# Two of three exp readings summed by an accumulating DMA before TensorE reads them, in an attention kernel

## The chip, the core and the metric

The kernel runs on one core of a Trainium2 chip. The time is device microseconds (us) of one execution. The kernel before takes 669.34 us, the median of three runs (669.19 to 669.51).

## What is computed

A transformer block with one key and one value head for 32 query heads of 20 columns each, in parallel with a feed-forward block, over 2048 rows of 640 columns in bfloat16:

```python
xn = _layernorm(x, axis=-1)
q = (xn @ wq).reshape(B, S, H, Dh).transpose(0, 2, 1, 3)   # H = 32, Dh = 20
k = xn @ wk                                               # one head, shared
v = xn @ wv
p = _softmax(einsum("bhqd,bkd->bhqk", q, k) * Dh ** -0.5, axis=-1)
o = einsum("bhqk,bkd->bhqd", p, v).transpose(0, 2, 1, 3).reshape(B, S, H * Dh) @ wo
return x + o + einsum("bsf,fd->bsd", silu(einsum("bsd,df->bsf", xn, w1)), w2)
```

## The kernel before

**Blocks.** The scores are cut into 2048 blocks of 128 keys by 512 queries, each of them one matmul that fills one bank of PSUM (L1127, called S here). Four heads of one query chunk make a group; there are 32 groups of 64 blocks. An S step is three or four blocks at once, since TensorE runs matmuls of 32 rows beside each other in its four row strips.

**Three ways to exp.** A block is turned into exp values in one of two ways. ScalarE reads two or three neighbouring banks and writes exact exps in bfloat16 (L1161, an E block). Or VectorE turns the scores of one bank into 16-bit integers whose bits, read as bfloat16, are a rough exp (L1176, a Z block). The rough reading is made better by averaging three of them: GpSimd adds two constants to the bit patterns of up to three Z blocks at a time (L1202, 64-bit integer adds that hold four 16-bit values each), which gives two shifted readings Y0 and Y1, each weighted by its own copy of V (`PH`: shifts 0, 43, 86; weights 1.0, 0.8046875, 0.625).

**PV.** Each reading is a matmul against V (L968, called PV), into one of the four 32-column strips of the group's accumulator U, so four of them run beside each other as one set. An E block costs one PV, a rough block three: one for Z, one each for Y0 and Y1. With 732 rough blocks that is 2048 + 2 x 732 = 3512 matmuls.

**The rest.** When a group is done, VectorE copies U out of PSUM (L1245), a DMA on SyncE's queue transposes it (L1216), VectorE takes the reciprocal of the row sums (L1231) and multiplies (L1236, called the product of U). The layer norm, K and V stand at the start (V's copies are made at L1804). The feed-forward block, the query projections and the output projection are spread between the attention steps as jobs (matmuls at L870; ScalarE's tanh at L1336; VectorE's L1341, L1294, L1405, L1424). Where a projection's query rows go to their places, SyncE's queue issues small transfers (L1303).

**What sets the order.** Every engine runs a fixed list of instructions, made at build time by a list scheduler (class `Sched`). It holds a cost for each operation and a latency for each hand-over. TensorE's choice is made in `step`: an S step when enough PSUM banks are free and ScalarE is about to run out, else PV sets or jobs. A table `SEG` holds 28 numbers for each 32 or so blocks of progress (how far VectorE may be behind before it gets no more blocks, when PV is preferred, and so on). `flush_z` hands a filled triple of Z blocks to GpSimd; `normalise` makes the reciprocal and the product of U. Waits between engines are on semaphores, in the order of the lists: an engine whose next instruction waits holds up all that stand behind it. Buffers go round: 35 E blocks, 8 triples of Z, 4 pairs of triples of Y.

Of the kernel before, what the change touches and what calls it, by code (L numbers as in the profile page):

```python
# [16 lines left out]
P = 128  # L17
# [18 lines left out]
UT_LATE = 2.0  # L36
UT_LATE1 = 4.0
# [8 lines left out]
PH = ((0, 1.0), (43, 0.8046875), (86, 0.625))  # L46
# [4 lines left out]
NBLK = 35  # L51
NZ = 8
NY = 4
QS = 6
ZB = 3
# [49 lines left out]
YP_FIX = 0.147  # L105
YP_BLK = 0.218
# [13 lines left out]
            "ACT4", "SPLIT", "U2", "LOOK", "W4", "M3")  # L120
SEG = (
# [105 lines left out]
class Sched:  # L227
# [59 lines left out]
    def ready(self, op, extra=0.0):  # L287
# [17 lines left out]
        if op.lock:  # L305
            r = max(r, self.lock_end["pool" if op.eng == "dve" else "dve"])
# [1576 lines left out]
```

## Time and profile before

One execution was profiled. Its own time is 669.12 us; the span from its first to its last instruction is 667.3 us, so 1.8 us lie around it, and it stands 0.22 us below the median.

| what | value |
|---|---|
| median of three runs | 669.34 us |
| the profiled execution | 669.12 us, span 667.3 us |
| first exp starts, last exp ends | 18.51 us, 654.08 us |
| busy: TensorE, ScalarE, VectorE, GpSimd | 659.4, 647.7, 601.3, 404.6 us |
| PV matmuls, S matmuls | 3512, 2048 |
| blocks exped by ScalarE, by VectorE | 1316, 732 |
| integer adds on GpSimd | 492 |

In the tables of the profile, PE is TensorE (PEld its weight loads), DVE VectorE, ACT ScalarE, POOL GpSimd and SP SyncE. A group's row reads: line, engine, operation, output from input, shapes, count, then busy time and the mean duration of one, then the engine's idle time before them and what ended it. Instructions on one engine overlap by their pipelines, so the mean duration is longer than the step from one to the next. The chain of waits is followed back from the last instruction; a row of it is start, length, and what ran.

### The profile page before, as it was taken

How to read it: one execution, taken by the hardware profiler on the slowest of the kernel's cores; microseconds unless marked ns; L12 is line 12 of the kernel's file. 1: busy time of each engine (PE TensorE's matmuls, PEld its weight loads, DVE VectorE, ACT ScalarE, POOL GpSimd, SP SyncE). 2: the span in 40 equal slices, each digit the busy share in tenths (PEclk: the TensorE clock that was granted, in tenths of full speed). 3: DMA queues.
4: the chain of work that ended last, by engine and by line, in shares of the span. 5: the costliest groups of instructions: out<-in, count | busy, mean ns of one | idle time of the engine just before them, and what ended most of it. 6: DMA issues, size and time to landing. Idle time of an engine off the chain costs nothing.

```text
span 667.3 us, 22800 instructions
## 1 busy us (share of the span) xinstructions
PE 659.4 (99%) x9735; PEld 220.4 (33%) x9735; DVE 601.3 (90%) x1085; ACT 647.7 (97%) x737; POOL 404.6 (61%) x509
## 2 busy tenths in 40 slices
PE   8999999999999999999999999999999999999998
PEld 4432233332323322233333323233233333223345
DVE  7888999999989999999889999988999999998783
ACT  7999999999999999999999999999999999999993
POOL 2056457777486656676556653866767674676550
PEclk9999999999999999999999999999999999999999
DMA  7565201010012210000003110000002121001001
GB/s 211 110 213 150 73 14 12 2 26 2 18 44 62 57 10 17 3 10 18 19 10 84 41 32 17 10 10 18 10 13 47 38 57 37 10 10 31 5 11 41
DMA packets 51433, 26.73 MB, mean 40 GB/s; under 512 B 38566, under 2 KB 50694, under 8 KB 51334
## 3 DMA queue, kind: packets, MB, share of 16 engines
q1 hardware_dynamic: 51190, 25.12, 14.5%
q8 instruction: 78, 1.28, 0.8%
q14 instruction: 21, 0.17, 0.1%
q10 hardware_dynamic: 144, 0.16, 0.1%
HBM read 11.44 MB, written 2.62 MB: 21 GB/s over the span
## 4 chain that ended last, share of the span: by engine, by line
PE 87%; ACT 7%; DVE 3%; SPq 1%; DMA 1%; issue 0%; ACTq 0%
PE psall L968 33%; PE psall L1127 28%; PE psall L870 26%; ACT sbt L1161 6%; DVE sbt L1176 2%; ACT sbt L1336 1%; SPq L1531 1%; DMA sbt<-in_A_x_dram 1%; DVE sbt L1424 0%; PE psall L1326 0%; DVE sbt L1236 0%; ACT sbt L1620 0%; DVE sbt L1666 0%; DVE sbt L1771 0%; ACT sbt L1655 0%
## 5 line engine op out<-in xcount | busy, mean ns | idle before, releaser
L1161 ACT ACTIVATE sbt<-psall 128x1024 bf16<-128x1024 f32 (+2 forms) x649 | 620.1, 1129 | 3.5 <-PE psall L1127 2.6
L1202 POOL INT64_ADD sbt<-sbt x492 | 399.7, 827 | 244.4 <-DVE sbt L1176 171.3
L1176 DVE TENSOR_SCALAR sbt<-psall 128x512 uint16<-128x512 f32 x732 | 473.1, 683 | 46.3 <-PE psall L1127 37.1
L968 PE MATMUL psall<-sbt 128*32 128x512 bf16 x3512 | 265.0, 383 | 0.2
L1127 PE MATMUL psall<-sbt 32*128 32x512 bf16 x2048 | 245.8, 384 | 2.1 <-ACT sbt L1161 0.7
L870 PE MATMUL psall<-sbt 128*32 128x320 bf16 (+2 forms) x3923 | 220.7, 331 | 0.5 <-DVE sbt L1176 0.4
L1127 PEld LDWEIGHTS psall<-sbt 32*128 32x128 bf16 x2048 | 61.9, 91 | 241.4 <-ACT sbt L1161 161.1
L870 PEld LDWEIGHTS psall<-sbt 128*32 128x32 bf16 x3923 | 84.6, 95 | 84.6 <-issue 54.4
L968 PEld LDWEIGHTS psall<-sbt 128*32 128x32 bf16 x3512 | 64.4, 95 | 101.3 <-issue 64.6
L1336 ACT ACTIVATE sbt<-psall 128x512 bf16<-128x512 f32 x54 | 39.6, 739 | 0.0
L1341 DVE SCALAR_TENSOR_TENSOR sbt<-sbt,psall 128x512 bf16<-128x512 bf16 x54 | 36.6, 682 | 2.6 <-ACT sbt L1336 1.2
L1245 DVE CAST sbt<-psall 128x512 bf16<-128x512 f32 x32 | 21.8, 681 | 5.4 <-PE psall L968 5.3
L1236 DVE TENSOR_TENSOR sbt<-sbt 128x320 bf16<-128x320 bf16 x31 | 18.3, 591 | 0.1
L846 PE MATMUL psall<-sbt 128*128 128x512 bf16 (+4 forms) x55 | 15.2, 428 | 1.2 <-DVE sbt L1590 1.2
L1424 DVE SCALAR_TENSOR_TENSOR sbt<-psall,sbt 128x320 bf16<-128x320 f32 x28 | 13.1, 477 | 2.9 <-PE psall L870 2.9
L1405 DVE SCALAR_TENSOR_TENSOR sbt<-psall,sbt 128x320 bf16<-128x320 f32 x28 | 13.5, 483 | 1.6 <-PE psall L870 1.4
L1294 DVE TENSOR_SCALAR sbt<-psall 128x512 bf16<-128x512 f32 (+1 forms) x19 | 12.9, 680 | 0.1
L1635 DVE BATCH_NORM_STATS2 sbt<-sbt 128x6 f32<-128x320 bf16 x22 | 10.0, 470 | 0.9 <-DMA sbt<-in_A_x_dram 0.7
L1421 ACT ACTIVATE sbt<-psall 128x320 bf16<-128x320 f32 x4 | 1.7, 438 | 8.7 <-PE psall L870 8.7
L846 PEld LDWEIGHTS psall<-sbt 128*128 128x128 bf16 x55 | 5.5, 109 | 9.1 <-issue 4.0
L1231 DVE RECIPROCAL sbt<-sbt 128x16 f32<-128x16 bf16 x31 | 7.5, 243 | 0.0
L1620 ACT ACTIVATE sbt<-sbt 128x640 bf16<-128x640 bf16 x5 | 3.6, 730 | 3.2 <-DMA sbt<-in_A_x_dram 3.2
(57 smaller groups left out, 70.1 us busy)
## 6 DMA issues: line engine op xcount, KB each, us to landing
sbt<-in_A_x_dram SPq DMA_DIRECT2D x32, 160.0 KB, 3.2
out_dram<-sbt SPq DMA_DIRECT2D x15, 160.0 KB, 2.0
sbt<-in_B_w_dram SPq DMA_DIRECT2D x5, 432.0 KB, 5.3
sbt<-sbt SPq DMA_DIRECT2D x105, 20.0 KB
sbt<-in_B_w_dram SPq DMA_DIRECT2D x13, 160.0 KB, 3.1
sbt<-sbt SPq DMA_TRANSPOSE x58, 2.5
sbt<-in_A_wo_dram SPq DMA_DIRECT2D x5, 160.0 KB, 3.1
sbt<-in_A_wq_dram SPq DMA_DIRECT2D x5, 140.0 KB, 3.1
```

The costliest lines, as they stand in the source:

```text
L846: return pe.matmul(self.bk(b, 0, n), self.zero[:, 0:P], self.zero[:, 0:n], start=True, stop=True)
L870: ins = pe.matmul(self.bk(b, 0, n, r, r + SLOT), w[:, r:r + SLOT], x, start=start, stop=stop, tile_position=(0, r), skip_group_check=True)
L968: ins = pe.matmul(self.bk(ub[k], 0, QW, r, r + SLOT), self.v[:, it.w, it.kt, :], it.x(), start=f, stop=False, tile_position=(0, r), skip_g ...
L1127: ins = pe.matmul(self.bk(bank[x]), self.kT[r:r + SLOT, kt * P:(kt + 1) * P], self.qT[r:r + SLOT, g % QS, :], start=True, stop=True, tile_ ...
L1161: return a.activation(self.E[:, b0 * QW:(b0 + na) * QW].rearrange("p (b n) -> p b n", n=QW), src, AF.Exp, scale=ACT_SCALE)
L1176: return v.tensor_scalar(self.Z[:, zs, zp * QW:(zp + 1) * QW], self.bk(bb), OFF, ZMAX, ALU.add, ALU.min)
L1202: sc.new("pool", YP_FIX + YP_BLK * n, lambda g, k=k: g.int64_add(self.Y[:, ys, k, 0:w].bitcast(I64), self.Z[:, zs, 0:w].bitcast(I64), PH[k ...
L1236: sc.new("dve", t_dve_ps(16 * DH), lambda v: v.tensor_tensor(dst, ut[:, :, :, 0:DH], rb, ALU.mult), [key, ("rL", up)], [("o", h0 + i) for ...
L1245: sc.new("dve", t_dve_ps(QW), lambda v: v.tensor_copy(self.U[:, up, :], self.bk(ub)), [("B", ub)], [("U", up)], prio=U_PRIO, name=f"Uev{g}")
L1336: sc.new("act", t_act(QW), lambda a: a.activation(t, src, AF.Tanh, scale=0.5), [("B", b)], [("tb", tp)], prio=TH_PRIO, name=f"th{c}_{fk}") ...
L1341: sc.new("dve", t_dve_ps(QW), lambda v: v.scalar_tensor_tensor(out=self.hT[0:rows, fk, :], in0=t, scalar=1.0, in1=src, op0=ALU.add, op1=AL ...
L1405: sc.new("dve", t_dve_ps(320), lambda v: v.scalar_tensor_tensor(out=in1, in0=ps, scalar=0.5, in1=in1, op0=ALU.mult, op1=ALU.add), [("B", b ...
```

## The change

Four things change together, and the lists are planned anew with a new table.

1. **Two copies of V.** The shifts become 39 and 82, and both shifted readings have the same weight (`VW = (1.0, 0.71875)`), so Y0 and Y1 are used with the same copy of V. VectorE makes two copies instead of three.
2. **Merged triples.** For full triples where GpSimd is planned to be less than `MG` us behind (a number of the table, 0 to 4), after 78 us and not near the end of a group, GpSimd issues a DMA that adds Y1 to Y0 in place, in bfloat16, 384 KB at a time. TensorE then reads one sum instead of Y0 and Y1: three matmuls instead of six for the triple. The scheduler counts 0.9 us for the issue, 5.7 us from the start of the issue to the landing, and 0.28, 0.22 and 0.12 us more for the three adds behind it.
3. **The product of U kept apart from GpSimd.** The product waits by semaphore for GpSimd's last add, GpSimd's next add waits for the product, and the scheduler holds GpSimd back when a product is about to be ready.
4. **Other numbers.** Later due times for U's transposes (2.0 to 3.8 us) and for the query transfers (+1.8 us); 36 E blocks, 6 triples of Z, 5 pairs of triples of Y; the table's 64 rows get new numbers and a 29th column.

```diff
-PH = ((0, 1.0), (43, 0.8046875), (86, 0.625))
+SHIFT = (39, 82)
+VW = (1.0, 0.71875)
+NRM = 0.42
+ACC_ISSUE = 0.9
+ACC_LAND = 5.7
+ACC_NEXT = (0.28, 0.22, 0.12)
+ACC_FROM = 78.0
+ACC_DMA = 1.8
+MG_END = 16
-UT_LATE = 2.0
+UT_LATE = 3.8
-NBLK = 35
-NZ = 8
-NY = 4
+NBLK = 36
+NZ = 6
+NY = 5
 SEG = (
-    (6.04, 3.723, 0.711, 0.248, 4, 4, 5, 1.38, 0.05, 0, 2.56, 6, 2.29, 0.4, 10, 6, 6, 54, 15, 31, 2, 0, 0, 1, 99, 0, 0, 1),
+    (4.38, 0.382, 0.113, 0.226, 4, 5, 1, 1.298, 0.05, 4.33, 2.053, 16, 2.57, 1.281, 10, 6, 10, 54, 15, 33, 8, 0, 0, 3, 99, 0, 0, 1, 2),
...
@@ commit
             if e == "dve":
                 self.last_add = op
-            self.lock_end[e] = op.end + (0.2 if e == "dve" else 0.0)
+                if op.name[:3] == "nrm" and self.last_pool is not None and self.last_pool.end > start - KEEP:
+                    op.deps.add(self.last_pool)
+            elif not op.dma:
+                self.last_pool = op
+            self.lock_end[e] = op.end + (0.2 if e == "dve" else 0.5 if op.dma else 0.2)
@@ flush_z
+        merge = n == ZB and back < MG and sc.t["pe"] > ACC_FROM and self.bp < GB * (g1 + 1) - MG_END
         for k in range(2):
-            sc.new("pool", YP_FIX + YP_BLK * n, lambda g, k=k: g.int64_add(
+            yp = sc.new("pool", YP_FIX + YP_BLK * n, lambda g, k=k: g.int64_add(
...
+            yp.lock = True
+        if merge:
+            op = sc.dma("pool", lambda g: g.dma_start(
+                self.Y[:, ys, 0, 0:w].bitcast(BF16), self.Y[:, ys, 1, 0:w].bitcast(BF16), accum_op=ALU.add),
+                [("Y", ys, 1, i) for i in range(n)], [("Y", ys, 0, i) for i in range(n)], P * w * 2,
+                sem=self.acc_sem[ys], prio=3.9, name="acc")
...
         for i, (t, g, kt, j) in enumerate(self.zblocks):
-            for k in range(2):
-                self.item(g, j, kt, k + 1, lambda k=k, i=i: self.Y[:, ys, k, i * QW:(i + 1) * QW].bitcast(BF16),
-                          [("Y", ys, k, i)])
+            for k in range(1 if merge else 2):
+                self.item(g, j, kt, 1,
+                          lambda k=k, i=i: self.Y[:, ys, k, i * QW:(i + 1) * QW].bitcast(BF16), [("Y", ys, k, i)])
```

In the code of the change S is at L1160, PV at L1001, the jobs at L903, ScalarE's exps at L1194, the Z blocks at L1209, the adds at L1238, the new DMA at L1244, the product of U at L1287. The list of each engine shows what moved. Counted over the whole lists: 96 triples are merged; VectorE has 736 blocks instead of 732; PV is 2048 + 2 x 736 - 3 x 96 = 3232 matmuls; ScalarE exps 1312 blocks, in 634 instructions of two banks, 9 of three and 17 of one (before: 565, 51 and 33); the S steps are 641 runs instead of 626; GpSimd has 502 adds (472 of a full triple) instead of 492; fill matmuls that only keep TensorE warm (L846) go from 55 to 49.

GpSimd's list from the first small triples on (a triple is 128x768, two blocks 128x512, one 128x256), before:

```order
L1202 ISA sbt<-sbt 128x768 x14
L1750 MEMSET sbt 128x640
L1202 ISA sbt<-sbt 128x768 x8
L1202 ISA sbt<-sbt 128x256 x2
L1202 ISA sbt<-sbt 128x768 x30
L1202 ISA sbt<-sbt 128x512 x2
```

And the same place of the changed program:

```order
L1238 ISA sbt<-sbt 128x768 x12
L1803 MEMSET sbt 128x640
L1238 ISA sbt<-sbt 128x768 x10
L1238 ISA sbt<-sbt 128x256 x2
L1238 ISA sbt<-sbt 128x768 x10
L1244 DMA sbt<-sbt 128x1536
L1238 ISA sbt<-sbt 128x768 x4
L1238 ISA sbt<-sbt 128x512 x2
```

Where GpSimd had adds alone, a DMA issue now stands behind the second add of a merged triple, and later adds queue behind it.

TensorE's list around the first merged triple, changed program. The first row is the S step that gave VectorE the last of the triple's three blocks; the last row begins with the matmul that waits for the DMA's landing:

```order
L1160 MATMUL psall<-sbt 128x512 x3
L1001 MATMUL psall<-sbt 32x512 x8
L1160 MATMUL psall<-sbt 128x512 x3
L1001 MATMUL psall<-sbt 32x512 x8
L1160 MATMUL psall<-sbt 128x512 x4
...
L1160 MATMUL psall<-sbt 128x512 x3
L1001 MATMUL psall<-sbt 32x512 x16
L1160 MATMUL psall<-sbt 128x512 x4
L1001 MATMUL psall<-sbt 32x512 x8
```

Between the two stand ten S steps and nine runs of PV or jobs with 22 sets of four.

The end of TensorE's list, from the last S step on (32x320 matmuls at L870 or L903 are the feed-forward and output projections), before:

```order
L1127 MATMUL psall<-sbt 128x512 x2
L968 MATMUL psall<-sbt 32x512 x18
L870 MATMUL psall<-sbt 32x320 x8
L968 MATMUL psall<-sbt 32x512 x2
L870 MATMUL psall<-sbt 32x320 x20
L968 MATMUL psall<-sbt 32x512 x2
L870 MATMUL psall<-sbt 32x320 x28
L1252 MATMUL psall<-sbt 128x128 x4
L870 MATMUL psall<-sbt 32x320 x56
L1368 MATMUL psall<-sbt 128x128 x4
L870 MATMUL psall<-sbt 32x320 x176
```

And changed:

```order
L1160 MATMUL psall<-sbt 128x512 x4
L1001 MATMUL psall<-sbt 32x512 x25
L903 MATMUL psall<-sbt 32x320 x16
L1001 MATMUL psall<-sbt 32x512 x2
L903 MATMUL psall<-sbt 32x320 x32
L1304 MATMUL psall<-sbt 128x128 x4
L903 MATMUL psall<-sbt 32x320 x40
L1421 MATMUL psall<-sbt 128x128 x4
L903 MATMUL psall<-sbt 32x320 x88
```

The same matmuls exist in all, but 112 of the 288 projection matmuls that stood behind the last S step now stand ahead of it.

In VectorE's list, 30 of the 31 products of U now wait for GpSimd's semaphore as well; before, none did. Of the Z blocks one waits for GpSimd to have read its buffer.

More of the change, by code (lines that the diff above doesn't have):

```diff
@@ L35 @@
 UBANK = 7
-UT_LATE = 2.0
-UT_LATE1 = 4.0
+UT_LATE = 3.8
+UT_LATE1 = 5.0
 BANKS = (6, 0, 1, 2, 3, 4, 5)
@@ L45 @@
 OFF = 16045.0
-PH = ((0, 1.0), (43, 0.8046875), (86, 0.625))
+SHIFT = (39, 82)
+VW = (1.0, 0.71875)
+NRM = 0.42
+NRM_SOON = 0.3
+NRM_PRIO = -2.0
+ACC_ISSUE = 0.9
+ACC_LAND = 5.7
+ACC_RATE = 165e3
+ACC_NEXT = (0.28, 0.22, 0.12)
+ACC_FROM = 78.0
+ACC_DMA = 1.8
+MG = 3.0
+MG_END = 16
 ZMAX = 32512.0
@@ L104 @@
 Y0_COST = 1.3294
-YP_FIX = 0.147
-YP_BLK = 0.218
+YP_FIX = 0.159
+YP_BLK = 0.222
 LIB = 0.2
@@ L119 @@
             "ZWAIT", "Y0_POOL", "Y0_COST", "JOB_BURST", "TILE_CAP", "E_HIGH", "Q_LEAD", "U_GO", "U_Z", "JU_E", "STRETCH",
-            "ACT4", "SPLIT", "U2", "LOOK", "W4", "M3")
+            "ACT4", "SPLIT", "U2", "LOOK", "W4", "M3", "MG")
 SEG = (
[64 rows of a table removed]
[64 rows of a table added]
 )
@@ L244, in __init__ @@
         self.dmaq = defaultdict(float)
+        self.after_acc = 99
+        self.last_pool = None
     def sem(self, name):
@@ L306, in ready @@
             r = max(r, self.lock_end["pool" if op.eng == "dve" else "dve"])
+            if op.eng == "pool":
+                for d in self.pend["dve"]:
+                    if d.lock and d.name[:3] == "nrm" and all(x.avail is not None and x.avail <= self.t["pool"] + NRM_SOON
+                                                              for x in d.deps):
+                        r = max(r, self.t["dve"] + d.dur)
         return r
@@ L312, in commit @@
             op.on_pick(op)
+        if e == "pool":
+            if op.dma:
+                self.after_acc = 0
+            else:
+                if self.after_acc < len(ACC_NEXT):
+                    op.dur += ACC_NEXT[self.after_acc]
+                self.after_acc += 1
         op.start = start
@@ L319, in commit @@
             else:
-                op.avail = max(op.end + 2.0, q + op.mode / 375e3) + op.late
+                op.avail = max(op.end + 2.0, q + op.mode / (ACC_RATE if op.name == "acc" else 375e3)) + op.late
             self.dmaq[e] = max(q, op.avail - op.late)
@@ L518, in alloc @@
         self.kT = sb([P, S], BF16)
-        self.v = sb([P, 3, KT, SLOT], BF16)
+        self.v = sb([P, 2, KT, SLOT], BF16)
         self.qT = sb([P, QS, QW], BF16)
@@ L594, in steps_init @@
         self.yset = 0
+        self.merged = 0
+        self.acc_no = [0] * NY
+        self.acc_sem = [self.sc.sem(f"acc{i}") for i in range(NY)]
         self.zblocks = []
@@ L1200, in flush_z @@
         w = n * QW
+        g1 = self.zblocks[-1][1]
+        back = max(sc.t["pool"] - sc.t["pe"], 0.0) + sum(o.dur for o in sc.pend["pool"])
+        merge = n == ZB and back < MG and sc.t["pe"] > ACC_FROM and self.bp < GB * (g1 + 1) - MG_END
         for k in range(2):
-            sc.new("pool", YP_FIX + YP_BLK * n, lambda g, k=k: g.int64_add(
+            yp = sc.new("pool", YP_FIX + YP_BLK * n, lambda g, k=k: g.int64_add(
                 self.Y[:, ys, k, 0:w].bitcast(I64), self.Z[:, zs, 0:w].bitcast(I64),
-                PH[k + 1][0] * 0x0001000100010001), zk + [("lib",)], [("Y", ys, k, i) for i in range(n)],
+                SHIFT[k] * 0x0001000100010001), zk + [("lib",)], [("Y", ys, k, i) for i in range(n)],
                 prio=4.0, name=f"yp{k}")
+            yp.lock = True
[4 more added lines that the diff above has]
+                sem=self.acc_sem[ys], prio=3.9, name="acc")
+            op.dur = ACC_ISSUE
+            op.lock = True
+            op.late = ACC_LAND - 2.0 - ACC_ISSUE
+            self.acc_no[ys] += 1
+            op.inc_no = self.acc_no[ys]
+            self.merged += 1
+            for _, g, kt, j in self.zblocks:
+                self.nz[g][j] -= 0.5
         for i, (t, g, kt, j) in enumerate(self.zblocks):
-            for k in range(2):
-                self.item(g, j, kt, k + 1, lambda k=k, i=i: self.Y[:, ys, k, i * QW:(i + 1) * QW].bitcast(BF16),
-                          [("Y", ys, k, i)])
+            for k in range(1 if merge else 2):
+                self.item(g, j, kt, 1,
+                          lambda k=k, i=i: self.Y[:, ys, k, i * QW:(i + 1) * QW].bitcast(BF16), [("Y", ys, k, i)])
             self.g_late[g] -= 1
@@ L1235, in normalise @@
         rb = bass.AP(self.rL, rl.offset, [list(rl.ap[0]), list(rl.ap[1]), [1, 4], [0, DH]])
-        sc.new("dve", t_dve_ps(16 * DH), lambda v: v.tensor_tensor(
+        last = g == self.NG - 1
+        op = sc.new("dve", NRM, lambda v: v.tensor_tensor(
             dst, ut[:, :, :, 0:DH], rb, ALU.mult), [key, ("rL", up)], [("o", h0 + i) for i in range(4)],
-            prio=U_PRIO if g < self.NG - 1 else -1.0, name=f"nrm{g}")
+            prio=-1.0 if last else NRM_PRIO, name=f"nrm{g}")
+        op.lock = not last
         self.norm_made[g // 8] += 4
@@ L1306, in consume @@
                 ops[-1].dur = 0.74
+                ops[-1].late = ACC_DMA if sc.t["pe"] > ACC_FROM else 0.0
             sc.note(ops[-1], (), [("q", c, h, lo) for h in heads])
@@ L1597, in prologue @@
         pool(1.4, lambda g: g.memset(self.v[:, :, :, :], 0.0), [("idb",), ("id2",)], [("v0",)] + [("v", i) for i in range(8)])
-        for k in range(3):
-            pool(0.15, lambda g, k=k: g.memset(self.v[:, k, :, DH:DH + 1], 0.5 * PH[k][1]), [("v0",)],
+        for k in range(2):
+            pool(0.15, lambda g, k=k: g.memset(self.v[:, k, :, DH:DH + 1], 0.5 * VW[k]), [("v0",)],
                  [("v0",)] + [("v", i) for i in range(8)])
@@ L1802, in consume @@
                 sv = self.bk(b, 0, 20 * m).rearrange("p (i d) -> p i d", d=DH)
-                for k in range(3):
+                for k in range(2):
                     sc.new("dve", 0.07 + m * DH / 960.0, lambda v, k=k: v.tensor_scalar(
-                        self.v[:, k, n0:n1, 0:DH], sv, PH[k][1], None, ALU.mult),
+                        self.v[:, k, n0:n1, 0:DH], sv, VW[k], None, ALU.mult),
                         [("B", b), ("v0",)], [(kk, i) for i in range(n0 // 2, n1 // 2) for kk in ("v", "vv")], prio=0.6,
```

126 rows, old and new, of the table SEG are left out of this document.

## The prediction

> **What bounds the kernel now.** I read the page first, then the chain of waits, then the groups by form, then the windows. The page's first lines show no single bound:
>
> ```profile
> span 667.3 us, 22800 instructions
> PE 659.4 (99%) x9735; PEld 220.4 (33%) x9735; DVE 601.3 (90%) x1085; ACT 647.7 (97%) x737; POOL 404.6 (61%) x509
> PE 87%; ACT 7%; DVE 3%; SPq 1%; DMA 1%; issue 0%; ACTq 0%
> ```
>
> TensorE is busy 99% and carries 87% of the chain. Busy time of pipelined matmuls says little, so I look at pieces of the chain near the end, and at two others (start, length, what ran):
>
> ```profile
> 18.51 18.32 ACT sbt L1161 x18
> 253.80 12.83 ACT sbt L1161 x14
> ...
> 645.20 0.55 PE psall L968 x8
> 646.07 0.98 PE psall L968 x16
> 647.92 0.32 PE psall L1127 x3
> 648.24 0.76 PE psall L968 x12
> 651.61 0.32 PE psall L1127 x2
> 655.81 2.02 PE psall L870 x56
> ```
>
> From 8 to 12 to 16 PV matmuls the run grows by 0.21 and 0.22 us: a set of four costs 0.216, and changing to it and back to S adds about 0.11 to a run. An S step of two or three blocks costs 0.32 whatever is in it. A set of the 320-column jobs costs 2.02 / 14 = 0.144. These pieces follow each other without a pause, so TensorE really is full where the chain lies on it. It is not alone:
>
> ```profile
> L1161 ACT ACTIVATE sbt<-psall 128x1024 bf16<-128x1024 f32 x565 | 543.3, 1112 | 2.4 <-PE psall L1127 1.4 <-PE psall L968 0.3
> L1161 ACT ACTIVATE sbt<-psall 128x1536 bf16<-128x1536 f32 x51 | 76.3, 1526 | 1.1 <-PE psall L1127 1.1
> 57.12 0.63 ACT L1336 ACTIVATE sbt<-psall 128x512 bf16<-128x512 f32 x1
> 57.60 2.90 ACT L1161 ACTIVATE sbt<-psall 128x1024 bf16<-128x1024 f32 x3
> 563.07 1.12 ACT L1161 ACTIVATE sbt<-psall 128x1024 bf16<-128x1024 f32 x1
> 563.97 0.70 ACT L1336 ACTIVATE sbt<-psall 128x512 bf16<-128x512 f32 x1
> 642.93 11.15 ACT L1161 ACTIVATE sbt<-psall 128x1536 bf16<-128x1536 f32 x12 [0.50 <-PE psall L1127]
> 78.00:628.00 550.00, 548.96 (x8159) 175.27 (x8157) 510.61 (x859) 547.71 (x609) 359.65 (x443) 1.00 0.10 24
> ```
>
> The last row is the window from 78 to 628 us: PE, PEld, DVE, ACT and POOL busy, granted clock, DMA share. ScalarE is busy 547.71 of 550. But one exp lasts 1112 ns while the next may start after 0.90 (563.07 to 563.97), so a delay of up to 0.2 us between two hides under the tail of the first. At start-to-start costs of 0.90 for two banks, 0.48 for one (57.12 to 57.60) and 0.90 + (1526 - 1112) ns = 1.32 for three, the exps and tanhs need 565 x 0.90 + 51 x 1.32 + 33 x 0.48 + 54 x 0.48 = 617.5 us. They take from 18.51 to 642.93 + 11.15 = 654.08, that is 635.6: some 18 us of hidden room. Not all can be had: where the chain lies on ScalarE itself it runs 14 in 12.83, 0.916 each, 1.8% above 0.90, which is 11 us over 617. So 7 us of ScalarE's time is won by a quicker TensorE, at most. Two engines are full together, with VectorE at 510.61 of 550 as a near third. GpSimd has 190 us to spare in that window.
>
> **The change part by part.** *PV.* 96 merged triples take 288 matmuls out, four more blocks on VectorE put 8 in. By the runs in the two lists, sets of four fall from 889 to 828: 61 x 0.216 = -13.2 us. But the S steps grow from 626 runs to 641, each 0.32 and a turn of 0.11: 15 x 0.43 = +6.5. Six fills less: -1.3. TensorE's sum: -8.0 us.
>
> *ScalarE.* 634 x 0.90 + 9 x 1.32 + 17 x 0.48 + 54 x 0.48 = 616.6, so -0.9 us: the change hardly takes work from it. Behind the last S step, where ScalarE has nothing left, 112 of 288 projection matmuls are gone, 28 sets x 0.144 = -4.0, against 5 more PV matmuls, +0.3. So ScalarE's path (start, exps, end) is shorter by 0.9 + 3.7 = 4.6 us if its hidden room stays as it is; the projections that moved forward run beside exps, and are in TensorE's sum.
>
> *VectorE.* The rows:
>
> ```profile
> L1176 DVE TENSOR_SCALAR sbt<-psall 128x512 uint16<-128x512 f32 x732 | 473.1, 683 | 46.3 <-PE psall L1127 37.1
> L1236 DVE TENSOR_TENSOR sbt<-sbt 128x320 bf16<-128x320 bf16 x31 | 18.3, 591 | 0.1
> L1236 DVE TENSOR_TENSOR sbt<-sbt x31: 471/483/1072, 60.8 to 640.3; 128x320 bf16<-128x320 bf16 x31
> L1804 DVE TENSOR_SCALAR sbt<-psall 128x80 bf16<-128x80 f32 x12 | 2.8, 233 | 0.1
> L1202 POOL INT64_ADD sbt<-sbt x492 | 399.7, 827 | 244.4 <-DVE sbt L1176 171.3 <-PE psall L968 69.5 <-PE psall L1127 1.6
> PEld psall L968 <- POOL sbt L1202: 15.9, 69, 0.3
> ```
>
> Four blocks more cost 4 x 0.65 = +2.6, four copies of V less give 0.9. The product of U has median 483 and mean 591 ns, up to 1072: some of the 31 are stretched, and kept apart they give 31 x 0.108 = -3.3 us. The new wait costs between nothing (GpSimd is already idle) and one add of 0.83 each, 26 us, and while VectorE waits, Z blocks queue behind it, and TensorE's next S step behind the banks they hold. The scheduler holds GpSimd back for a coming product, so I take a fifth, +5. VectorE's sum is +3, inside the 39 us it has free in the window, spread thin.
>
> The Trainium skill (SBUF — State Buffer, Who interferes with whom) states that a VectorE operation with two SBUF inputs and a GpSimd operation that reads SBUF exclude each other for a whole instruction, whichever is second. The longest product, 1072 ns, is 0.59 above the median and so less than one whole add of 0.83; by the rule alone each collision would cost up to 0.83 and the parting would give up to 26 us rather than 3.3. I stay with the row.
>
> *GpSimd and the merge.* The trace has no DMA issued by GpSimd and none that adds. The nearest rows:
>
> ```profile
> L1303 SPq DMA_DIRECT2D sbt<-sbt x135: 558/707/1261, 44.4 to 565.4; - x135
> sbt<-sbt SPq DMA_DIRECT2D x1, 512.0 KB, 3.7
> sbt<-in_B_w_dram SPq DMA_DIRECT2D x13, 160.0 KB, 3.1
> L1216 SPq DMA_TRANSPOSE sbt<-sbt x31: 1189/1209/1976, 55.3 to 636.2; - x31
> DMA to landing us min/median/max: 2.3/2.4/4.1
> 565.93 11.25 POOL L1202 INT64_ADD sbt<-sbt  x14 [6.01 <-PE psall L968]
> 566.72 9.81 DVE L1176 TENSOR_SCALAR sbt<-psall 128x512 uint16<-128x512 f32 x15
> ```
>
> An issue is 0.56 to 1.26 us on SyncE's queue: 96 of them are 54 to 121 us of GpSimd's time, beside its 190 free, so GpSimd does not become the bound. I count them at the scheduler's 0.9. Plain transfers of 160 and 512 KB land in 3.1 and 3.7 us; 384 KB would take 3.5, of which about 0.65 grows with size. An adding transfer also reads its destination: at least that growing part again, 4.1; at four times it, 5.4. So, from the S step: its 0.39, the Z block 0.68, two adds 2 x 0.80 (14 in 11.25), issue 0.9, landing 3.5 to 5.4, in all 7.1 to 9.0 us, and small waits between. TensorE's work from that step to the first reader, for the triple in the list: 10 S steps and 22 sets at 0.216, 19 turns of 0.105, is 8.9 us; by the same count over all 96 the median is 9.6, the tightest tenth under 7.8, the least 7.2. So a landing up to about 5 us costs nothing but at the tightest tenth: at 5.4 ten readers wait 1 us, +10. A landing at the plain price costs nothing. I take 4.1 to 5, and +1 us for the tight ones.
>
> The Trainium skill (DMA: Bandwidth & Descriptors, Anatomy of one DMA) gives GpSimd-issued transfers 2.0 us plus bytes at 436 per ns, an estimate of 2.9 us for 384 KB. By it no reader would wait; nothing there prices the adding, and no row of the trace before shows it.
>
> *Transposes and queries.* They share the DMA engines with 96 x 384 KB. U's transpose lands in 2.4 us (median), and the reciprocal behind it is in VectorE's list; it now stands 1.8 us later by plan. Nothing if the delay is under that.
>
> **The sum.** If TensorE decides everywhere, -8.0; if ScalarE with its room unchanged, -4.6. Both are full, and the chain changes between them. Tail and -0.9 are sure to both; in the middle TensorE has -4.3 to give and ScalarE 7 us of room to take it. I take -7.0, seven tenths of the way from the one to the other, and +1 for late merges: -6.0. The profiled 669.12 becomes 663.1, and with its 0.22 below the median 663.3 us.
>
> **Rivals.**
> *ScalarE alone.* Its room is jitter, no effect of TensorE, and the new lists are no better at the turns: -4.6 and the +5 of VectorE's waits shows in part, so 665 to 669. For it: only 0.9 us of its work goes. Against: 87% of the chain is TensorE.
> *Late merges (slower).* The adding transfer, or one behind the queries' transfers, lands later than the lists expect, in order-bound TensorE. It decides from a landing of about 5.5 us after the issue. Merges come about every 5.7 us and a window from S to reader is 9.6 us, so 56 windows follow each other in 540 us: each us beyond costs up to 56, at half of the windows 28. With 1 us late: 663 + 28 = 691; with only the tightest tenth late, 673. Against: today TensorE waits at most 0.3 us for an add, 15.9 in all.
> *Starved issue.* If VectorE's Z blocks, which run nearly without a pause, kept GpSimd from issuing, each issue would wait for one or more of them, 0.65 us each, and the landing would slip past the readers as above: 680 to 700. Against: 14 adds at 0.80 ran beside 15 Z blocks back to back, so Z blocks block no write of GpSimd. The Trainium skill (SBUF — State Buffer, SBUF: two separate sides) warns of such a thing: GpSimd cannot write a DMA's descriptors while VectorE runs an operation that holds the port they share. The row speaks against its being met here.
> *VectorE's new waits.* U's transposes come late by 1 us, or products wait a whole add: 31 us against 39 free; a quarter shows, 663 + 8 = 671.
> That nothing is merged is ruled out by the list: 96 issues stand in it.
>
> **How the numbers follow.** Forecast 0.68 (659 to 667); ScalarE alone 0.12, of which 0.05 is within 0.2%; late merges 0.12; starved issue 0.03; VectorE's waits 0.05, split 0.01 faster, 0.03 same, 0.01 slower. About 0.2%, 1.3 us, is what a measurement of this kernel can tell. Faster: 0.68 + 0.07 + 0.01 = 0.76. Same: 0.08. Slower: 0.12 + 0.03 + 0.01 = 0.16. The low end takes TensorE's -8.0 with VectorE's 3.3 shown as well, 658. The high end takes in VectorE's waits and stops short of late merges, 672; some 0.13 lies above it.
>
> **What would show it.** Right: PV 3232 in some 244 us busy; exps from 18.5 to about 651.5; behind the last S step 9 instead of 12.5 us; products of U near 0.48 each; waits of weight loads at PV for the DMA under 5 us in all. Wrong: a row of PV waiting for the merge with tens of us; GpSimd's adds with many waits behind the issue; reciprocals waiting for transposes; ScalarE with idle time of over 10 us.

## The result and the profile after

The changed kernel takes 664.51 us (median of four runs, 663.79 to 664.74), the kernel before, timed beside it, 669.42 (669.19 to 669.51). The ratio is 0.9925, with a 95% interval of 0.9913 to 0.9937: 4.9 us less, where 6.0 less was forecast. The profiled execution took 664.74 us, 4.38 less than the profiled one of before.

The page's first lines and the shares of the chain, after:

```profile
span 662.9 us, 22421 instructions
PE 652.1 (98%) x9446; PEld 215.2 (32%) x9449; DVE 601.2 (91%) x1085; ACT 645.8 (97%) x748; POOL 488.0 (74%) x614
PE 61%; ACT 35%; DVE 2%; DMA 1%; SPq 0%; issue 0%
```

TensorE's share of the chain fell from 87% to 61%, and ScalarE's rose from 7% to 35%. That reads as if TensorE had got some room; the experiments below show that this reading is only half right.

Where the 4.4 us of span went can be read from ScalarE's first and last exp (start, length, what ran):

```profile
18.61 1.02 ACT L1194 ACTIVATE sbt<-psall 128x1024 bf16<-128x1024 f32 x1 [1.09 <-PE psall L1160]
637.74 15.35 ACT L1194 ACTIVATE sbt<-psall 128x1024 bf16<-128x1024 f32 x16
```

The exps ran from 18.51 to 654.08 before, 635.6 us, and run from 18.61 to 637.74 + 15.35 = 653.09 now, 634.5 us: 1.1 less. From there to the end of the span it was 667.3 - 654.1 = 13.2 us and is 662.9 - 653.1 = 9.8. So three quarters of the gain lie behind the last exp. The windows of just that stretch, first of before (columns: window, its length, then PE, PEld, DVE, ACT and POOL busy with their instructions, granted clock, DMA share, GB/s):

```profile
654.08:667.30 13.22, 10.16 (x276) 7.36 (x270) 6.08 (x14) 1.69 (x5) 0.00 (x0) 1.00 0.15 52
```

And after:

```profile
653.08:662.90 9.82, 6.77 (x173) 4.79 (x170) 5.17 (x12) 1.70 (x5) 0.00 (x0) 1.00 0.19 68
```

TensorE runs 103 matmuls less there and is busy 3.39 us less: this is the whole of the 3.40 us by which the stretch is shorter. The stretch repeats: in the profiles of the runs below that leave the end alone it is 13.2 to 13.4 us with the old lists and 9.8 with the new ones. By the medians (4.9 us) some 1.5 us are then left for all that stands ahead, where the two profiled executions show 1.0; the profiled one of after is the slowest of its four, the only one with a granted clock below 1.00 (0.997), and the clock stands at 0.66 between 25 and 30 us in it. The middle, 78 to 628 us, hardly changed; after:

```profile
78.00:628.00 550.00, 548.00 (x8069) 175.31 (x8061) 510.67 (x863) 547.09 (x618) 440.90 (x544) 1.00 0.47 91
```

TensorE 548.0 against 549.0, ScalarE 547.1 against 547.7, VectorE 510.7 against 510.6. GpSimd is the one that took on work, 81 us, and the DMA engines' share went from 0.10 to 0.47.

The groups that the change touches (line, engine, operation, count, then busy and mean ns, then idle before them and what ended it):

```profile
L1194 ACT ACTIVATE sbt<-psall 128x1024 bf16<-128x1024 f32 (+1 forms) x660 | 617.9, 1105 | 4.8 <-PE psall L1160 4.4
L1238 POOL INT64_ADD sbt<-sbt x502 | 428.5, 975 | 123.6 <-DVE sbt L1209 87.3
L1209 DVE TENSOR_SCALAR sbt<-psall 128x512 uint16<-128x512 f32 x736 | 478.8, 684 | 42.1 <-PE psall L1160 32.6
L1001 PE MATMUL psall<-sbt 128*32 128x512 bf16 x3232 | 250.6, 383 | 0.4 <-DVE sbt L1394 0.4
L1244 POOL DMA_DIRECT2D sbt<-sbt x96 | 88.1, 918 | 39.1 <-DVE sbt L1287 29.4
L1287 DVE TENSOR_TENSOR sbt<-sbt 128x320 bf16<-128x320 bf16 x31 | 14.9, 481 | 0.0
```

And what waits for what at the new places (waiting engine and line, releaser, us in total, times, longest):

```profile
POOL sbt L1238 <- DVE sbt L1287: 29.7, 16, 3.0
POOL sbt L1244 <- DVE sbt L1287: 29.4, 14, 3.1
PEld psall L1001 <- POOL sbt L1238: 6.1, 27, 0.2
```

No row has PV (L1001) waiting for the adding transfer. One row has other work of TensorE waiting for another transfer, a transpose of the attention output (L1408, on SyncE's queue), once, at 515 us; before, no matmul of the jobs (L870) waited for a DMA:

```profile
PE psall L903 <- DMA sbt<-sbt: 1.2, 1, 1.2
```

The product of U starts without idle time (0.0 in its row); the price of keeping it apart is paid by GpSimd, which waits 29.7 + 29.4 us for it. The transfers themselves, from their issue to their landing:

```profile
L1244 POOL DMA_DIRECT2D sbt<-sbt x96: 827/874/1330, 81.9 to 640.3; - x96
...
DMA to landing us min/median/max: 3.8/4.3/6.2
```

### The profile page after: what moved, and what is told of

Its sections match the earlier page's. It is cut to its first block, busy times and chain, and to the rows that moved or that the text cites. A ratio compares the mean times of both kernels' runs of the same rounds, so it can differ in the third digit from the quotient of the medians.

```text
span 662.9 us, 22421 instructions
## 1 busy us (share of the span) xinstructions
PE 652.1 (98%) x9446; PEld 215.2 (32%) x9449; DVE 601.2 (91%) x1085; ACT 645.8 (97%) x748; POOL 488.0 (74%) x614
## 3 DMA queue, kind: packets, MB, share of 16 engines
q0 software_dynamic: 13824, 37.75, 30.7%
## 4 chain that ended last, share of the span: by engine, by line
PE 61%; ACT 35%; DVE 2%; DMA 1%; SPq 0%; issue 0%
ACT sbt L1194 32%; PE psall L1001 23%; PE psall L1160 20%; PE psall L903 17%; ACT sbt L1389 3%; DMA sbt<-sbt 1%; DVE sbt L1688 1%; DMA sbt<-in_A_x_dram 1%; PE psall L1379 0%; DVE sbt L1209 0%; DVE sbt L1719 0%; SPq L1584 0%; DVE sbt L1477 0%; DVE sbt L1824 0%; DVE sbt L1394 0%
## 5 line engine op out<-in xcount | busy, mean ns | idle before, releaser
L1194 ACT ACTIVATE sbt<-psall 128x1024 bf16<-128x1024 f32 (+1 forms) x660 | 617.9, 1105 | 4.8 <-PE psall L1160 4.4
L1238 POOL INT64_ADD sbt<-sbt x502 | 428.5, 975 | 123.6 <-DVE sbt L1209 87.3
L1209 DVE TENSOR_SCALAR sbt<-psall 128x512 uint16<-128x512 f32 x736 | 478.8, 684 | 42.1 <-PE psall L1160 32.6
L1160 PE MATMUL psall<-sbt 32*128 32x512 bf16 x2048 | 252.2, 385 | 2.5 <-DVE sbt L1839 1.1
L1001 PE MATMUL psall<-sbt 128*32 128x512 bf16 x3232 | 250.6, 383 | 0.4 <-DVE sbt L1394 0.4
L903 PE MATMUL psall<-sbt 128*32 128x320 bf16 (+2 forms) x3923 | 225.9, 333 | 1.4 <-DMA sbt<-sbt 1.2
L1160 PEld LDWEIGHTS psall<-sbt 32*128 32x128 bf16 x2048 | 63.2, 91 | 246.0 <-ACT sbt L1194 184.1
L1244 POOL DMA_DIRECT2D sbt<-sbt x96 | 88.1, 918 | 39.1 <-DVE sbt L1287 29.4
L903 PEld LDWEIGHTS psall<-sbt 128*32 128x32 bf16 x3923 | 82.5, 95 | 88.1 <-issue 57.5
L1001 PEld LDWEIGHTS psall<-sbt 128*32 128x32 bf16 x3232 | 60.1, 95 | 94.0 <-issue 70.2
L1287 DVE TENSOR_TENSOR sbt<-sbt 128x320 bf16<-128x320 bf16 x31 | 14.9, 481 | 0.0
L879 PE MATMUL psall<-sbt 128*128 128x512 bf16 (+4 forms) x46 | 12.5, 421 | 1.6 <-DVE sbt L1643 1.2
L1458 DVE SCALAR_TENSOR_TENSOR sbt<-psall,sbt 128x320 bf16<-128x320 f32 x28 | 13.4, 480 | 0.2 <-PE psall L903 0.2
```

Source lines behind the costliest of these rows:

```text
L879: return pe.matmul(self.bk(b, 0, n), self.zero[:, 0:P], self.zero[:, 0:n], start=True, stop=True)
L903: ins = pe.matmul(self.bk(b, 0, n, r, r + SLOT), w[:, r:r + SLOT], x, start=start, stop=stop, tile_position=(0, r), skip_group_check=True)
L1001: ins = pe.matmul(self.bk(ub[k], 0, QW, r, r + SLOT), self.v[:, it.w, it.kt, :], it.x(), start=f, stop=False, tile_position=(0, r), skip_g ...
L1160: ins = pe.matmul(self.bk(bank[x]), self.kT[r:r + SLOT, kt * P:(kt + 1) * P], self.qT[r:r + SLOT, g % QS, :], start=True, stop=True, tile_ ...
L1194: return a.activation(self.E[:, b0 * QW:(b0 + na) * QW].rearrange("p (b n) -> p b n", n=QW), src, AF.Exp, scale=ACT_SCALE)
L1209: return v.tensor_scalar(self.Z[:, zs, zp * QW:(zp + 1) * QW], self.bk(bb), OFF, ZMAX, ALU.add, ALU.min)
```

## The experiments

The theories: **TensorE decides** (its freed time is the gain), **ScalarE decides** (its work and the end are the gain, the rest is jitter), **both are full together** (each hides most of what the other gains). The last three runs ask whether a gain is paid back by the transfers, and what the semaphores are worth.

| run | what is different | us | ratio to before (95%) |
|---|---|---|---|
| after | the change | 664.51 | 0.9925 (0.9913-0.9937) |
| b_pv_cut | before, 58 PV sets cut | 667.87 | 0.9978 (0.9968-0.9988) |
| b_act_cut | before, 16 exps halved | 668.08 | 0.9982 (0.9973-0.9992) |
| b_both_cut | before, both | 664.70 | 0.9932 (0.9915-0.9948) |
| a_act_cut | after, 16 exps halved | 664.55 | 0.9928 (0.9910-0.9946) |
| a_both_cut | after, 52 PV sets and 16 exps | 660.29 | 0.9864 (0.9850-0.9879) |
| b_tail_cut | before, 28 sets before the last transposes | 668.01 | 0.9976 (0.9967-0.9986) |
| b_tail2_cut | before, 22 sets of the last row | 667.24 | 0.9966 (0.9953-0.9979) |
| b_fill | before, 33 sets more | 672.90 | 1.0050 (1.0035-1.0065) |
| a_fill | after, 31 sets more | 669.95 | 1.0012 (1.0002-1.0021) |
| a_no_dma | after without the transfers | 663.88 | 0.9914 (0.9899-0.9928) |
| a_no_lock | after without the semaphore waits | 682.72 | 1.0205 (1.0160-1.0251) |
| a_no_lock_no_dma | after without both | 664.08 | 0.9931 (0.9911-0.9950) |

**One engine relieved, in the kernel before.** 58 sets of PV in the middle become one matmul of 32 columns each:

```diff
+        cut = self.npv % 14 == 0 and 78 < sc.t["pe"] < 640 and not any(first)
...
+            if cut:
+                it, k = items[-1]
+                r = it.tile * SLOT
+                return pe.matmul(self.bk(ub[k], 0, 32, r, r + SLOT), self.v[:, it.w, it.kt, :], it.x()[:, 0:32], ...)
```

> The kernel before with its lists unchanged; 58 PV sets between 78 and 640 us, one in 14, do a single matmul of 32 columns in place of up to four of 512 (those readings are left out). That takes 58 x 0.19 = 11 us from TensorE in the middle and nothing from ScalarE, VectorE or the end. If TensorE sets the pace in the middle (the prediction's step, which let it give 2 to 4 us of its 4.3 there): -4 to -11 us. If ScalarE's list does, with its 15 us of hidden room being jitter at the hand-overs: 0 to -1.5 us.

And 16 exps of two banks read one bank:

```diff
+            short = na == 2 and self.nex > 70 and self.nex % 36 == 0
...
+                if short:
+                    return a.activation(self.E[:, b0 * QW:(b0 + 1) * QW], self.bk(run[0]), AF.Exp, scale=ACT_SCALE)
```

> The kernel before with its lists unchanged; 16 of the two-bank exps, spread from about 85 us on, exp one bank only (the other 16 blocks keep old values): 16 x 0.43 = 6.8 us less of ScalarE, the same TensorE. If ScalarE sets the pace in the middle: -4 to -7 us. If TensorE does: 0 to -2 us. Both engines full: in between, and then less than half.

11 us taken from TensorE (58 x 0.19; its busy time fell by 7.1) gave 1.4; 6.8 us taken from ScalarE (16 x 0.43; busy 4.1 less) gave 1.2. Each engine alone gives a tenth to a fifth of what it is relieved of. The chain of b_pv_cut:

```profile
ACT 63%; PE 30%; DVE 5%; issue 1%; DMA 1%; SPq 0%
```

The bound passed from TensorE to ScalarE after little more than one us. In b_act_cut the chain stayed where it had been:

```profile
PE 87%; ACT 7%; DVE 4%; DMA 1%; SPq 0%; issue 0%
```

**Both relieved, before and after.** The same two edits together (in the changed kernel 52 sets, since it has fewer):

> The kernel before with unchanged lists and both cuts at once: 58 PV sets reduced to one matmul of 32 columns (11 us less of TensorE) and 16 two-bank exps to one bank (6.8 us less of ScalarE). Alone they gave 1.4 and 1.2 us. If the two engines are full together and each alone hides behind the other, both at once give far more than 2.6: -5 to -6.5 us (ScalarE's cut nearly whole). If a third, VectorE with its order-bound list, holds both: -2 to -3 us.

> The changed kernel with unchanged lists and both cuts (52 PV sets, 10 us of TensorE; 16 exps, 6.8 us of ScalarE). Full together: -4 to -6.5 us against 664.5, about 659. A third engine as the bound: 0 to -2 us, 662.5 to 664.5.

Before, 4.6 us: somewhat under the 5 to 6.5 expected, but 2.0 more than the two single gains together. After, 4.2 us, to 660.29. The changed kernel with ScalarE alone relieved:

> The changed kernel with its lists unchanged and the same cut of 16 two-bank exps to one bank, 6.8 us less of ScalarE. If ScalarE sets the pace there (its chain share rose from 7% to 35%): -5 to -7 us against the changed kernel's 664.5, about 658.5. If TensorE still did: 0 to -2 us. In either case the cut should be worth more here than in the kernel before, since TensorE has 8 us less to do.

It gave nothing that can be measured (664.55 against 664.51; its four runs lie between 663.17 and 666.05), where more than in the old kernel had been expected, and the chain swung back to TensorE:

```profile
PE 84%; ACT 11%; DVE 1%; DMA 1%; SPq 1%; issue 0%; ACTq 0%
```

So in the old kernel both engines are full together. In the changed one the cuts show that ScalarE alone does not set the pace; the cut of PV alone was not run there. That ScalarE is still as full rests on its 35% of the chain and its 547.1 busy us of 550, and is argued, not shown. Even both cuts bring less than the smaller of them (4.6 and 4.2 us of 6.8): what comes third, VectorE or the fixed lists, was not tried.

**The end.** Two runs cut projection sets behind the last S step of the old kernel to 32 columns, first 28 sets from the rows ahead of the last transposes, then 22 sets in the last row of TensorE's list. The edit of the second (the first picks its jobs by other names):

```diff
+        if self.bp >= NB and job.name[:3] in ("G2_", "G3_", "F12", "F13") and begun:
+            self.ncut = getattr(self, "ncut", 0) + 1
+            cut = self.ncut <= 22
...
+        if self.cut and not start:
+            n, x = 32, x[:, 0:32]
```

> The kernel before with its lists unchanged; 28 of the 72 sets of projection matmuls behind the last S step do 32 columns in place of 320 (their other columns are left out), about 28 x 0.11 = 3 us less of TensorE where nothing else runs. Both theories: -2.5 to -3.5 us; under -1.5 us the end would not be TensorE's, and the gain of the change would have to come from the middle.

> The kernel before with unchanged lists; 22 of the 44 sets of projection matmuls in the last row of TensorE's list, behind the last transpose of the attention output, do 32 columns in place of 320 (the rest is left out): 22 x 0.107 = 2.35 us less. These stand where the changed kernel has 22 sets fewer. If the end is what the change won: -2.2 to -2.5 us. If something else (the last outputs' VectorE work or transfers) ends the kernel: 0 to -1 us, as the cut ahead of that transpose gave -1.3 of 3.0.

The first took 3.0 us of work out and gave 1.3, less than the 2.5 to 3.5 expected. Its timeline says why (start, length, what ran, idle before it and its releaser):

```profile
643.50 11.14 ACT L1174 ACTIVATE sbt<-psall 128x1536 bf16<-128x1536 f32 x12 [0.50 <-PE psall L1140]
...
654.70 0.39 PE L981 MATMUL psall<-sbt 128*32 128x512 bf16 x2 [0.41 <-ACT sbt L1174]
...
655.88 0.40 PE L1265 MATMUL psall<-sbt 128*128 128x128 bf16 x4 [0.50 <-DVE sbt L1258]
```

TensorE, with less to do, waits 0.41 us for the last exp and 0.50 for VectorE's copy: those sets were cover for the chain exp, PV, U, transposes. The last exp ends at 643.50 + 11.14 = 654.64, 0.56 us later than in the profile of before; these exps began 0.57 us later, so the difference lies ahead of the cut. Counted from there the end is 1.6 us shorter (13.2 to 11.6). The second cut took some 2.35 us from behind that chain and gave 2.0 (2.4 in its profile, 13.2 to 10.8). So work in TensorE's last row counts about in full, and work ahead of it by about half.

**TensorE given more.** Sets of four 320-column matmuls with zero weights are put between PV runs in the middle, about as much work as the moved projections:

```diff
+        more = self.npv % 23 == 0 and 78 < sc.t["pe"] < 640 and not any(first) and len(items) == 4
...
+                    ins = pe.matmul(self.bk(ub[items[0][1]], 0, 320, r, r + SLOT), self.zero[:, 0:SLOT], self.zero[:, 0:320], ...)
```

> The kernel before with unchanged lists and 33 additional sets of four 320-column matmuls with zero weights, behind PV sets between 78 and 640 us: 33 x 0.135 = 4.5 us more of TensorE, the sum is unchanged. It prices what it would have cost to move projections of the end (28 sets in the change) into the middle without merging. If TensorE is as full as ScalarE: +3 to +4.5 us. If ScalarE alone sets the pace and TensorE's room takes it: +0 to +1 us.

> The changed kernel with unchanged lists and 31 such sets, 4.2 us more of TensorE. The changed kernel's chain lies 35% on ScalarE, and its PV cut and exp cut together gave 4.2 us where the exp cut alone gave nothing, so I expect TensorE nearly as full: +1.5 to +3 us against 664.5. If the merges left TensorE with room in the middle: 0 to +1 us; if it is as full as before: as much as in the kernel before, +3 to +4.2.

33 sets, 4.5 us, cost the old kernel 3.5. 31 sets, 4.2 us, cost the changed one 5.4 (its ten runs lie between 668.34 and 671.52). The room of 4 us that the sum had found for TensorE in the middle is not there to be filled: the changed kernel is at least as sensitive as the old one. That it costs more than the sets last, and more than was expected in any case, is explained in part by its profile (671.23 us). The transpose that held TensorE for 1.2 us in the changed kernel holds it for 2.52 here, PV waits twice (0.5 and 1.3 us) for a merged sum, which it does not do in the profile of after, and the clock granted to TensorE falls behind the longest wait:

```profile
518.42 0.45 PE L903 MATMUL psall<-sbt 128*32 128x320 bf16 x8 [2.52 <-DMA sbt<-sbt]
520.00:525.00 5.00, 5.00 (x71) 1.39 (x63) 3.73 (x7) 3.86 (x5) 2.22 (x3) 0.77 0.05 13
```

The two of the ten runs with a clock of 1.00 over the whole took 668.34 and 670.05; the other eight, at 0.995 to 0.997, 669.63 to 671.52.

**The transfers left out.** The order of all else stays; PV reads the first shifted reading without the sum:

```diff
+            if op.name == "acc":
+                continue
+            deps = set()
             for d in op.deps:
+                deps |= d.deps if d.name == "acc" else {d}
+            for d in deps:
```

> The changed kernel with unchanged lists but without the 96 adding DMAs: a merged triple's readers wait for GpSimd's add and read Y0 alone (Y1 of those triples is left out). It takes away 88 us of GpSimd's issues, 37.75 MB of transfers and the wait for the landing. If the merge is hidden as the trace shows (no weight load of PV waits for it): -0.5 to +0.5 us against 664.5. If its traffic or GpSimd's later adds still cost something behind other waits: -1 to -3 us.

663.88 us against 664.51, and the intervals overlap: what the 96 issues and landings cost is 0.6 us or nothing. They do slow GpSimd's adds (mean 975 ns with, 810 without) and U's transposes (landing 3.7 us with, 2.3 without, medians), and both are hidden. Not hidden is TensorE's wait of 1.2 us for a transpose of the attention output: it is gone without the transfers.

**The semaphores left out.** Same lists, without the waits between the products of U and GpSimd's adds:

```diff
-            if e == "pool" and self.last_add is not None and self.last_add.end > start - KEEP:
+            if e == "pool" and self.last_add is not None and self.last_add.end > start - KEEP and start < 40.0:
...
-                    op.deps.add(self.last_pool)
+                    self.nolock.append((op, self.last_pool))
```

> The changed kernel with unchanged lists, but without the semaphore waits between the products of U and GpSimd's adds (both directions; the planned spacing stays). The products' mean should rise from 481 towards 591 ns, 31 x 0.11 = 3.4 us of VectorE, and GpSimd's 59 us of waits for products should go. If VectorE's time counts at the bound: +1 to +3 us. If VectorE has the room (about 40 us idle in the middle): 0 to +0.5 us. If the waits cost more than they save: -1 to 0.

This was the largest miss of the study: 682.72 us (four runs, 680.10 to 687.10), 18 more than with the waits and 13 more than before the change. The groups of this run:

```profile
L1288 DVE TENSOR_TENSOR sbt<-sbt 128x320 bf16<-128x320 bf16 x31 | 35.0, 1128 | 0.0
L1195 ACT ACTIVATE sbt<-psall 128x1024 bf16<-128x1024 f32 x634 | 602.4, 1078 | 20.5 <-PE psall L1161 19.2
L1161 PE MATMUL psall<-sbt 32*128 32x512 bf16 x2048 | 254.1, 388 | 13.4 <-DVE sbt L1210 9.7 <-DVE sbt L1395 1.1 <-DVE sbt L1748 0.6
```

The 31 products last 20 us more in all (35.0 against 14.9); the S matmuls wait for VectorE's Z blocks that queue behind them, and ScalarE waits for S. The timeline around one of the longest products, GpSimd's rows and then VectorE's:

```profile
118.81 0.87 POOL L1245 DMA_DIRECT2D sbt<-sbt  x1
119.42 2.73 POOL L1239 INT64_ADD sbt<-sbt  x3
...
119.43 0.63 DVE L1210 TENSOR_SCALAR sbt<-psall 128x512 uint16<-128x512 f32 x1
119.97 2.54 DVE L1288 TENSOR_TENSOR sbt<-sbt 128x320 bf16<-128x320 bf16 x1
```

The product starts in the first of three adds and ends at 122.51, 0.36 us after the third (119.42 + 2.73 = 122.15). It did not get in between the adds. Eleven of the 31 products (1.33 to 2.54 us) waited out two or three adds in this way, all of them beside a run of adds that began 0.60 to 0.73 us after the start of a transfer's issue. In the profile of before, products lasted 1.07 us at most. Either the transfers make the difference or the new lists do; the last run takes the transfers out of this kernel as well.

> The changed program's lists without the waits between products of U and GpSimd's adds, and also without the 96 adding transfers: TensorE reads the first shifted reading alone, so a third of each merged block's weight is left out. Without the waits alone the kernel took 682.72 us, the 31 products lasted 1.13 us on average and up to 2.54, each of the longest ending together with a run of two or three adds that had begun just behind a transfer's issue; without the transfers alone it took 663.88. Two readings. If it is the transfer that makes a product wait out more than one add (the adds behind an issue take 0.97 instead of 0.82 us and the product does not get in between them), then without transfers a product lasts as before the change, 0.59 on average and up to 1.07, and the kernel takes 664 to 668 us. If it is the adds alone, because the changed lists let a product begin in the middle of back-to-back adds, the products stay at 1.0 to 1.1 us on average, up to 2.5, and the kernel takes 676 to 684. I give the first 0.6.

664.08 us: without the transfers the waits are not missed. Its products:

```profile
L1293 DVE TENSOR_TENSOR sbt<-sbt x31: 473/485/1144, 56.0 to 647.3; 128x320 bf16<-128x320 bf16 x31
```

They have the durations of before again (471/483/1072 there). The longest of them beside its adds:

```profile
354.00 1.63 POOL L1244 INT64_ADD sbt<-sbt  x2 [1.49 <-DVE sbt L1215]
...
354.83 1.14 DVE L1293 TENSOR_TENSOR sbt<-sbt 128x320 bf16<-128x320 bf16 x1
```

It starts as the second add does (354.00 + 0.82) and ends at 355.97, 0.34 us after that add has ended at 355.63: it waited out one add. So a product that meets an add waits for one add in any case; with the transfers it waits for all that stand back to back behind an issue. The waits are needed because of the merge, more than for the 3.4 us that products lost before it.

The 18 us are not the products' time alone. In the profile (684.75 us, 20.0 more of span than after) TensorE pauses 12.2 us more, for instance 1.61 us behind the product of 162.59 us, and needs 7.8 us more of busy time (659.9 against 652.1) for the same matmuls. Behind four such pauses its granted clock is 0.66 to 0.72 for 5 us:

```profile
165.63 0.39 PE L1161 MATMUL psall<-sbt 32*128 32x512 bf16 x3 [1.61 <-DVE sbt L1210]
165.00:170.00 5.00, 4.37 (x60) 1.53 (x64) 3.36 (x6) 3.17 (x4) 0.00 (x0) 0.72 0.02 3
```

Some of the 18 us thus go with the clock: the two runs with a mean clock of 0.995 took 680.1 and 680.7, those with 0.987 and 0.985 took 684.8 and 687.1.

## Why the prediction was right, and where it was not

**TensorE's part, -8.0 us in the sum.** The counts held (3232 PV). Of the sum, the 28 sets that left the end were a gain (forecast -3.7 with the five matmuls more, measured -3.40). The rest, -4.3 in the middle, was not had. The step that failed is "I take -7.0, seven tenths of the way": it gave the middle 2.4 us beyond ScalarE's 0.9, and the whole middle gained 1.1 less 0.1 for the later start (some 1.5 by the medians). That forecast and result (-6.0 and -4.9) lie only 1.1 us apart owes something to luck: the +1 for late merges, which did not come, hid part of the miss. The 87% of the chain had seemed to speak for TensorE. b_pv_cut shows that such a share says who ends last, not by how much: 11 us less on that engine brought 1.4.

**ScalarE's path, -4.6 us.** Right in size: 0.9 + 3.7 forecast, 1.1 - 0.1 + 3.4 = 4.4 measured between the two profiled executions. Its hidden room is unchanged too: by the prediction's start-to-start costs 635.6 - 617.5 = 18.1 us before, 634.5 - 616.6 = 17.9 after. So the rival "ScalarE alone" (665 to 669, chance 0.12) had the better sum. But its ground, that TensorE has nothing to do with it, is refuted for the old kernel by the pair of cuts, and for both by the fills.

What the freed PV time bought is then this: the projections could move ahead of the last exp. b_fill gives 3.5 us as the cost of about as much TensorE work put into the old middle; the change moved 28 sets (4.0 us) there and its middle became no longer. That merging paid for the move fits all runs, but a plan with the move and without merging was not run.

**VectorE, +3 us.** The parting of the products gave what was said: 31 x 0.481 = 14.9 us against 18.3, that is -3.4 for -3.3. The +5 for the new waits was wrong in place: VectorE does not wait there (0.0 in its row), GpSimd does, and it has the time.

**The size of a collision.** "I stay with the row" was right for the kernel before and would have been wrong for the changed one, whose products without the waits last 20 us longer, not 3.3; without the transfers as well it is 3.6 (31 x 0.595 = 18.5 us against 14.9). The Trainium skill (SBUF — State Buffer, Who interferes with whom) has the two exclude each other for a whole instruction. Without transfers the runs agree: a product ends 0.34 us after the one add that it met. The prediction took its longest product, 0.59 above the median, as less than one add, but 0.34 us of the product run behind the add, so it was one. With transfers the runs go beyond the rule, up to three adds. Row and rule were no contradiction: the rule gives the largest size of a collision, and the row shows that 12 of the 31 old products had one (0.60 us or more), mostly with what was left of an add that had begun earlier.

**The merge, +1 us for late ones.** Landing was forecast at 4.1 to 5 us and is 4.3 (median, 6.2 at most), the issue at 0.9 and is 0.87 in the median (0.92 mean). By a_no_dma all of it costs 0.6 us or nothing. In the changed kernel late merges and a starved issue did not come; with 4.2 us more on TensorE (a_fill) PV did wait for a merge, twice. The estimate of 2.9 us from the Trainium skill (DMA: Bandwidth & Descriptors, Anatomy of one DMA) is 1.4 us short of the median landing.

**Transposes.** "Nothing if the delay is under" 1.8 us: the median landing rose by 1.3 us, from 2.4:

```profile
DMA to landing us min/median/max: 2.3/3.7/6.5
```

No wait of a reciprocal shows it. The prediction left out the 16 transposes of the attention output on the same queue: their longest landing went from 4.0 to 4.9 us, and one held TensorE for 1.2. **The other signs.** From the last S step to its last matmul TensorE takes 9.3 us, where it was 12.7. PV is busy 250.6 us, not 244 (265.0 before), the exps end at 653.1, not 651.5, and ScalarE is idle 4.8 us before its exps, well under 10.

## What to carry to other kernels

A chain that lies 87% on one engine tells nothing of the second one's distance: where two engines are busy 99% in the same window, count a gain in the middle only for what both are relieved of, and count about in full what leaves the last row of the engine that ends the program. Work freed on a full engine can still be spent: on moving work from the end into the middle, if someone pays for it there. Before a DMA is added beside a tuned pair of engines, ask which of their operations meet in SBUF, since a collision that cost 0.1 us on average before can cost 0.65 with the transfers running.

## What the runs showed of the hardware

- An adding transfer from SBUF to SBUF of 384 KB in bfloat16, issued by GpSimd, lands 3.8/4.3/6.2 us after its issue (least, median, most), and the issue holds GpSimd 0.87 us in the median; 96 of them fill 30.7% of the time of 16 DMA engines.
- GpSimd's adds take 934 (a_no_lock) to 975 ns on average beside them instead of 810 to 827, and DMA transposes on SyncE's queue land after 2.9 or 3.0 instead of 2.4 or 2.5 us (medians).
- A product of two SBUF operands on VectorE that meets an integer add on GpSimd ends 0.34 us after that add; when the adds follow an adding transfer's issue without a pause, it ends 0.36 us after the last of them. A transfer in flight is not enough: the products at 98.54 and 424.19 us of a_no_lock met adds that began 1.38 and 0.85 us after an issue's start, before its transfer can have landed (3.8 us at least in after), and waited out one add only. What the eleven have in common in the trace, whose spans on GpSimd are rough, is adds that overlap: the next one starts 0.15 to 0.36 us before the last has ended, where the two that got in met overlaps of 0.01 and 0.10, and in the three profiles without such transfers no two adds overlap by more than 0.03. So a product may need a moment without an add, which fits all runs and was not tested by itself. Why the adds behind an issue last longer (often 1.14 us instead of 0.83) is open.
- In the profile of a_no_lock TensorE paused six times for 1.44 to 1.81 us between 78 and 640 us. Behind four of these pauses the granted clock was 0.66 to 0.72 for 5 us, behind the other two (1.73 and 1.81 us) it stayed at 1.00; behind the pause of 2.52 us in a_fill it was 0.77. What decides it is not shown.
